# Decode attention and MLP on one core: K and V loaded four heads at a time, P turned among zeros, a shorter MLP chain

## The chip, the cores and the metric

The kernel runs on one core of a Trainium2 chip. The metric is the device time of one execution in microseconds; the median of three runs before the change is 203.85 us (202.43 to 204.0). All data starts and ends in HBM.

## The reference

One decode step for 8 sequences: a layer norm, attention over the last 2048 keys of a cache with 8 key heads (each shared by 4 query heads of 128), an output projection, and a two-part mixer and MLP. With sequence length 1, each of the four token shifts of the mixer moves its quarter of `h` out of range, so the term `hs` is zero, and `w1` and `w2` don't matter.

```python
W = min(4096, max(256, Sk // 4))           # 2048 of 8192 keys
q = (x @ wq) ...                            # 8 x 32 heads x 128
scores = einsum("bhqd,bhkd->bhqk", q, k) * Dh ** -0.5
o = einsum("bhqk,bhkd->bhqd", softmax(scores), v)
A = o.reshape(B, 1, 4096) @ wo

h  = x + A(layernorm(x))
u  = layernorm(h)                           # B's input
x1 = u                                      # the shifted term is zero
h2 = gelu(layernorm(x1) @ w3) @ w4          # 512 -> 1792 -> 512
out = h + x1 + h2
```

## The kernel before

**Items.** K and V are read once: 8 sequences x 8 key heads are 64 items, each with 512 KB of K and 512 KB of V. An item is loaded as 128 partitions of 4 KB (`load_k`, L362, `load_v`, L367): partition p holds the 16 consecutive keys 16p to 16p+15. There are `NK = 11` slots for K and `NV = 13` for V. All these loads go through SP's queue, and wait there for the turn (K) or the PV (V) that last used the slot.

**Turn and scores.** TensorE turns an item's K in 16 transposes of 128x128 (`pe_T`, L252) into one of two PSUM buffers; ACT copies the lower half to SBUF and VectorE the upper (`evict`, L260 and L262). `pe_QK` (L270) then runs four matmuls side by side on the four column groups, each with 32 stationary columns (`qblk`: four columns of this head's queries, the others zero) and 512 keys as moving columns. The 8 heads of a sequence accumulate into one PSUM tile `S_ps`: partitions are 4 quarters of keys times 32 query heads, columns 512 keys.

**Softmax.** After a sequence's eighth QK come the maximum over the columns (L279), a transpose of that to one row by a matmul (L283), the maximum over quarters and its negation (L285, L288), a matmul that turns it back into a column (L292), and Exp on ACT with the row sums beside it (L296, one instruction on 128 partitions x 512). Four transposes (L305) turn P, VectorE copies it (L309), and a matmul with ones adds up the row sums (L317), of which VectorE takes reciprocals (L319, L324).

**PV.** `pe_PV` (L331) runs 16 matmuls per item, V chunks as stationary operand and four columns of P as moving one. A sequence's heads 0 to 6 are scaled together into `oK` (L341), turned by four small matmuls against a selection matrix (L353) and copied to `o2` (L358); head 7 is scaled straight into `o2` (L345). The next sequence's PV waits for that copy, since it uses the same PSUM bank. In the last sequence each head has its own bank, its own turn, and its part of the output projection (`pe_wo`, L383, which starts with x as first summand).

**Order.** One loop over p (L391) writes the order out for every engine: turn p, then one of the softmax steps, then QK of item p-2, then PV of item p-13, with the loads of K p and V p-13 on SP. wo comes in five loads between items 15 and 39. After the loop SP has w3 and w4 (w4 in two parts, 1 KB runs).

**MLP (L459 to L522).** h lies transposed, 128 partitions of 4 x 8 columns. The mean comes from a fp32 matmul with ones and a reduction, h is centred, squared, and summed the same way. Two Sqrt on ACT and two reciprocals give both norms (the second norm of a norm is one factor: L470). u goes through w3 in two halves (L486), each followed by gelu written out in five DVE steps and a Tanh, then w4 (L508), the last sum, a transpose, a copy and the store.

Of the kernel before, what the change touches and what calls it, by code (L numbers as in the profile page):

```python
# [6 lines left out]
dt = mybir.dt  # L7
# [4 lines left out]
B = 8  # L12
D = 512
# [15 lines left out]
NK = 11  # L29
NV = 13  # L30
NKT = 4
LQK = 2
LV = 13
WO_AT = (15, 23, 31, 39)
# [32 lines left out]
def bass_sequential_preLN__sliding_block_cached__mixer_s_mlp__decode_kernel(  # L67
# [19 lines left out]
    NITEM = NB * G  # L87
# [3 lines left out]
    with es:  # L91
# [3 lines left out]


        iota_f = sb([128, 128], dt.float32, "iota_f")
# [3 lines left out]
        ones_f = sb([128, 128], dt.float32, "ones_f")  # L101
        scratch = sb([128, 2], dt.float32, "scratch")
        eps1 = sb([128, 1], dt.float32, "eps1")
        eps2 = sb([128, 1], dt.float32, "eps2")
# [8 lines left out]
        wbig = sb([128, KC * H * DH], dt.bfloat16, "wbig")  # L113
        wq_v = wbig[:, :].rearrange("p (k n) -> p k n", k=KC)

        wo_v = wbig[:, :].rearrange("p (g k n) -> p g k n", g=G, k=R)
        w3_sb = sb([128, KC, F], dt.bfloat16, "w3_sb")
        w4_sb = sb([128, FC, D], dt.bfloat16, "w4_sb")

        qblk = sb([128, B, G, H], dt.bfloat16, "qblk")  # L120
        knat = sb([128, NK, NC * DH], dt.bfloat16, "knat")
        vnat = sb([128, NV, NC * DH], dt.bfloat16, "vnat")
        kT_sb = sb([128, NKT, W], dt.bfloat16, "kT_sb")

        P_sb = sb([128, 2, 512], dt.bfloat16, "P_sb")
        pT_sb = sb([128, 2, NC, H], dt.bfloat16, "pT_sb")
# [7 lines left out]
        GL = G - 1  # L134
# [3 lines left out]
        oK = sb([128, G, R, R], dt.bfloat16, "oK")  # L138
# [3 lines left out]
        hs = sb([128, NH], dt.float32, "hs")  # L142
        hc = sb([128, NH], dt.float32, "hc")
        hsq = sb([128, NH], dt.float32, "hsq")
        msum = sb([128, B], dt.float32, "msum")
        vsum = sb([128, B], dt.float32, "vsum")
        s1 = sb([128, B], dt.float32, "s1")
        s2 = sb([128, B], dt.float32, "s2")
        r1 = sb([128, B], dt.float32, "r1")
        r2 = sb([128, B], dt.float32, "r2")  # L150
        xb = sb([128, NH], dt.float32, "xb")
        fin = sb([128, NH], dt.float32, "fin")
        uT = sb([128, NH], dt.bfloat16, "uT")
        g_x = sb([128, FC * B], dt.float32, "g_x")
        g_q = sb([128, FC * B], dt.float32, "g_q")
        g_t = sb([128, FC * B], dt.float32, "g_t")
        gT = sb([128, FC * B], dt.bfloat16, "gT")
        fT = sb([128, NH], dt.bfloat16, "fT")
# [3 lines left out]

# [3 lines left out]
        pT_ps = sm[:, 0:256].bitcast(dt.bfloat16)  # L166
# [6 lines left out]
        sem_v = [S(f"sem_v{i}") for i in range(NV)]  # L173
        sem_x, sem_wq, sem_wo, sem_w3, sem_w4a, sem_w4b, sem_out = (
# [8 lines left out]

# [3 lines left out]
        PO.op(lambda e: e.memset(eps1[:], EPS))  # L187
        e_eps = PO.op(lambda e: e.memset(eps2[:], EPS * EPS))
        e_iota = PO.op(lambda e: e.iota(iota_f[:], [[1, 128]], base=0, channel_multiplier=-1,
                                        allow_small_or_imprecise_dtypes=True))  # L190
        e_ones = PO.op(lambda e: e.memset(ones_f[:], 1.0))
        e_qz = PO.op(lambda e: e.memset(qblk[:], 0.0))
        e_warm = AC.op(lambda e: e.activation(scratch[:, 1:2], scratch[:, 0:1], ACT.Exp), e_scr)

        e_idb = DV.op(lambda e: e.tensor_single_scalar(ident_b[:], iota_f[:], 0.0, ALU.is_equal), e_iota)
        e_idf = DV.op(lambda e: e.tensor_single_scalar(ident_f[:], iota_f[:], 0.0, ALU.is_equal))
# [6 lines left out]
        e_sel = DV.op(lambda e: e.tensor_reduce(sel_f[:, :], ident_f[:, :].rearrange("p (q h) -> p h q", q=4),  # L203
# [6 lines left out]

        def pe_xT(e):
            for kc in range(KC):
                ins = e.matmul(pT_ps[:, kc * B:(kc + 1) * B],  # L213
                               xln_b[:, :].rearrange("b (p k) -> b k p", k=KC)[:, kc, :],
                               ident_b[0:B, 0:B], is_transpose=True)
            return ins
        e = PE.op(pe_xT, e_xln, e_idb)
        e_xT = DV.op(lambda e: e.tensor_copy(xlnT[:, :], pT_ps[:, 0:KC * B]), e)
# [11 lines left out]
        def dve_q(e):  # L230
            for g in range(G):
                ins = e.tensor_scalar(qblk[:, :, g, R * g:R * (g + 1)],  # L232
                                      S_ps[0][:, R * g * B:R * (g + 1) * B].rearrange("p (i b) -> p b i", b=B),
                                      inv_sqrt_dh, None, ALU.mult)
            return ins
        e_qblk = DV.op(dve_q, e_q, e_qz)


        e_Tlo, e_Thi, e_lo, e_hi, e_QK, e_PV = {}, {}, {}, {}, {}, {}
        e_max, e_mT, e_neg, e_negps, e_negc, e_exp, e_PT, e_pT, e_lsel, e_Lb, e_rL, e_scale, e_sc = ({} for _ in range(13))  # L240

        def K(i):
            return sem_k[i % NK], 16 * (i // NK + 1)

        def V(i):
            return sem_v[i % NV], 16 * (i // NV + 1)

        def pe_T(i):
            def half(lo):
                def f(e):  # L250
                    for c in range(lo, lo + NC // 2):
                        ins = e.matmul(kT_ps[i % 2][:, c * 128:(c + 1) * 128],  # L252
                                       knat[:, i % NK, c * DH:(c + 1) * DH], ident_b[:, :], is_transpose=True)
                    return ins
                return f
            e_Tlo[i] = PE.op(half(0), K(i), e_lo.get(i - 2), e_idb)
            e_Thi[i] = PE.op(half(NC // 2), e_hi.get(i - 2))

        def evict(i):
            e_lo[i] = AC.op(lambda e: e.activation(kT_sb[:, i % NKT, 0:W // 2], kT_ps[i % 2][:, 0:W // 2], ACT.Copy),  # L260
                            e_Tlo[i], e_QK.get(i - NKT))
            e_hi[i] = DV.op(lambda e: e.tensor_copy(kT_sb[:, i % NKT, W // 2:W], kT_ps[i % 2][:, W // 2:W]),  # L262
                            e_Thi[i], e_QK.get(i - NKT))

        def pe_QK(i):
            b, g = divmod(i, G)

            def f(e):
                for q in range(4):
                    ins = e.matmul(S_ps[b % 2][32 * q:32 * (q + 1), :], qblk[:, b, g, :],  # L270
                                   kT_sb[:, i % NKT, 512 * q:512 * (q + 1)],
                                   start=(g == 0), stop=(g == G - 1),
                                   tile_position=(0, 32 * q), skip_group_check=True)
                return ins
            e_QK[i] = PE.op(f, e_lo[i], e_hi[i], e_qblk, e_exp.get(b - 2))


        def softmax_1(b):
            e_max[b] = DV.op(lambda e: e.tensor_reduce(mcol[:, :], S_ps[b % 2][:, :], AX.X, ALU.max),  # L279
                             e_QK[G * b + G - 1], e_mT.get(b - 1))  # L280

        def softmax_2(b):
            e_mT[b] = PE.op(lambda e: e.matmul(sm[0:1, MROW], mcol[:, :], ident_f[:, :], start=True, stop=True),  # L283
                            e_max[b], e_rL.get(b - 1), e_idf)
            e = DV.op(lambda e: e.tensor_reduce(Mrow[:, :], sm[0:1, MROW].rearrange("o (q h) -> o h q", q=4),  # L285
                                                AX.X, ALU.max), e_mT[b])
            m_bc = bass.AP(tensor=Mrow[:, :].tensor, offset=0, ap=[[H, 1], [0, 4], [1, H]])
            e_neg[b] = DV.op(lambda e: e.tensor_scalar(negrow[:, :].rearrange("o (q h) -> o q h", q=4), m_bc,  # L288
                                                       -1.0, None, ALU.mult), e, e_negps.get(b - 1))

        def softmax_3(b):
            e_negps[b] = PE.op(lambda e: e.matmul(sm[:, NEG], negrow[0:1, :], ones_f[0:1, 0:1],  # L292
                                                  start=True, stop=True), e_neg[b], e_ones)
            j = b % 2
            e_negc[b] = DV.op(lambda e: e.tensor_copy(negcol[:, j:j + 1], sm[:, NEG]), e_negps[b], e_exp.get(b - 2))  # L295
            e_exp[b] = AC.op(lambda e: e.activation(P_sb[:, j, :], S_ps[j][:, :], ACT.Exp, bias=negcol[:, j:j + 1],  # L296
                                                    scale=1.0, accum_out=lcol[:, j:j + 1]),
                             e_negc[b], e_PT.get(b - 2), e_lsel.get(b - 2))

        def softmax_4(b):  # L300
            j = b % 2

            def f(e):
                for jt in range(4):
                    ins = e.matmul(pT_ps[:, jt * 128:(jt + 1) * 128], P_sb[:, j, 128 * jt:128 * (jt + 1)],  # L305
                                   ident_b[:, :], is_transpose=True)
                return ins
            e_PT[b] = PE.op(f, e_exp[b], e_negc[b])
            e_pT[b] = DV.op(lambda e: e.tensor_copy(  # L309
                pT_sb[:, j, :, :].rearrange("p (q jt) h -> p q jt h", jt=4),  # L310
                pT_ps[:, 0:NC * H].rearrange("p (jt q h) -> p q jt h", jt=4, q=4)),
                e_PT[b], e_PV.get(G * (b - 2) + G - 1))
            e_lsel[b] = DV.op(lambda e: e.tensor_scalar(lsel[:, :], sel_f[:, :], lcol[:, j:j + 1], None, ALU.mult),
                              e_Lb.get(b - 1), e_sel)

        def softmax_5(b):
            e_Lb[b] = PE.op(lambda e: e.matmul(sm[:, LB], ones_f[:, :], lsel[:, :], start=True, stop=True),  # L317
                            e_lsel[b], e_pT[b])
            e_r = DV.op(lambda e: e.reciprocal(rL[:, b % 2, :], sm[:, LB]), e_Lb[b],  # L319
                        e_scale.get(b - 2))  # L320
# [236 lines left out]
```

## Time and profile before

| | |
|---|---|
| median of three runs | 203.85 us |
| the profiled execution | 202.54 us |
| its span, first to last instruction | 201.1 us |
| mean granted TensorE clock | 0.829 |
| TensorE matmul busy | 156.3 us (78%) |
| VectorE, ACT busy | 76.5, 79.5 us |
| HBM read | 79.18 MB, 394 GB/s over the span |
| K transposes (L252), 1024 | 80.7 us busy |
| PV (L331), 1024 | 35.8 us busy |
| QK (L270), 256 | 30.2 us busy, four side by side |

A busy time of TensorE counts pipelined instructions whole, so it says when the engine is in use, not how close to its peak it is. The granted clock is the share of full speed that the clock throttle let through. A chain of waits is followed back from the last instruction, at each step to what released it; its lines are a start, a duration, an engine and a line.

### The profile page before, as it was taken

To read this page: it belongs to the slowest core of one execution; us is meant where nothing else is said; L and a number is where in the kernel's file an instruction comes from. 1 tells how busy PE (TensorE), PEld (TensorE's weight loads), DVE (VectorE), ACT (ScalarE), POOL (GpSimd) and SP (SyncE) were. 2 spreads that over 40 slices of the span, in tenths; PEclk is the share of its full clock that TensorE was granted. 3 is DMA by queue.
4 is the path that set the end of the run, shared out by engine and by line. 5 is a ranking of instruction groups with operands and counts; after the bars stand their busy time and mean duration, and the time that the engine had idled before them with its cause. 6 is when DMAs were issued, how large, how long until landed. Compare 5 with 4: busy or idle time off the path is not lost.

```text
span 201.1 us, 6188 instructions
## 1 busy us (share of the span) xinstructions
PE 156.3 (78%) x2821; PEld 126.0 (63%) x2821; DVE 76.5 (38%) x204; ACT 79.5 (40%) x91; POOL 2.5 (1%) x10
## 2 busy tenths in 40 slices
PE   0039999897876987678974898879798878979754
PEld 0039776676755765565863676657676666769753
DVE  6103556534441335213352246233524333234143
ACT  6003778744532444423432436444534523240030
POOL 4000000000000000000000000000000000000000
PEclk9999999999978797975799669996969975755555
DMA  6989999999999999999999999999999999999950
GB/s 223 476 364 418 420 416 421 415 415 418 416 420 416 421 415 415 421 416 420 418 409 413 420 417 419 417 416 418 417 420 416 415 420 421 415 418 416 393 179 2
DMA packets 22506, 79.59 MB, mean 396 GB/s; under 512 B 2248, under 2 KB 4560, under 8 KB 22352
## 3 DMA queue, kind: packets, MB, share of 16 engines
q1 hardware_dynamic: 22464, 79.18, 97.1%
q8 instruction: 22, 0.36, 0.6%
q10 hardware_dynamic: 16, 0.01, 0.0%
q14 instruction: 4, 0.03, 0.0%
HBM read 79.18 MB, written 0.01 MB: 394 GB/s over the span
## 4 chain that ended last, share of the span: by engine, by line
DMA 50%; PE 38%; DVE 6%; ACT 2%; issue 2%
DMA knat<-in_A_k_cache_dram 44%; PE kT_ps L252 19%; DMA wbig<-in_A_wq_dram 6%; PE S_ps L270 5%; PE oT_ps L331 4%; PE S_ps L383 2%; PE S_ps L225 2%; DVE kT_sb L262 1%; PE kT_ps L331 1%; PE sm L305 1%; PE sm L292 1%; ACT P_sb L296 1%; PE sm L283 1%; DVE mcol L279 1%; ACT L296 1%
## 5 line engine op out<-in xcount | busy, mean ns | idle before, releaser
L260 ACT ACTIVATE kT_sb<-kT_ps 128x1024 bf16<-128x1024 bf16 x64 | 65.5, 1023 | 95.1 <-PE kT_ps L252 95.0
L252 PE MATMUL kT_ps<-ident_b,knat 128*128 128x128 bf16 x1024 | 80.7, 243 | 12.0 <-DMA knat<-in_A_k_cache_dram 11.8
L252 PEld LDWEIGHTS kT_ps<-ident_b,knat 128*128 128x128 bf16 x1024 | 69.4, 110 | 16.7 <-DMA knat<-in_A_k_cache_dram 13.9
L262 DVE COPY kT_sb<-kT_ps 128x1024 bf16<-128x1024 bf16 x64 | 44.3, 692 | 92.7 <-PE kT_ps L252 92.6
L331 PEld LDWEIGHTS oT_ps<-pT_sb,vnat 128*128 128x128 bf16 x896 | 26.9, 98 | 27.4 <-issue 18.4
L331 PE MATMUL oT_ps<-pT_sb,vnat 128*128 128x4 bf16 x896 | 31.4, 165 | 11.2 <-DVE o L358 6.3
L270 PE MATMUL S_ps<-kT_sb,qblk 128*32 128x512 bf16 x256 | 30.2, 433 | 0.0
L270 PEld LDWEIGHTS S_ps<-kT_sb,qblk 128*32 128x32 bf16 x256 | 7.4, 95 | 5.6 <-issue 1.6
L225 PE MATMUL S_ps<-xlnT,wbig 128*128 128x8 bf16 x128 | 3.6, 168 | 7.7 <-DMA wbig<-in_A_wq_dram 7.7
L225 PEld LDWEIGHTS S_ps<-xlnT,wbig 128*128 128x128 bf16 x128 | 3.5, 104 | 7.8 <-issue 7.8
L296 ACT ACTIVATE P_sb<-S_ps,negcol 128x512 bf16<-128x512 f32 x8 | 5.5, 687 | 6.2 <-DVE negcol L295 6.2
L279 DVE TENSOR_REDUCE mcol<-S_ps 128x1 f32<-128x512 f32 x8 | 5.5, 682 | 1.4 <-PE S_ps L270 1.4
L470 ACT ACTIVATE s<-vsum,eps 128x8 f32<-128x8 f32 x1 | 0.3, 301 | 13.7 <-DVE vsum L467 13.7
L232 DVE TENSOR_SCALAR qblk<-S_ps 128x32 bf16<-128x32 f32 x8 | 0.9, 182 | 10.8 <-PE S_ps L225 10.8
L305 PE MATMUL sm<-ident_b,P_sb 128*128 128x128 bf16 x32 | 3.6, 242 | 1.7 <-ACT P_sb L296 1.7
L331 PE MATMUL kT_ps<-pT_sb,vnat 128*128 128x4 bf16 x128 | 4.4, 166 | 0.0
L383 PE MATMUL S_ps<-o,wbig 128*128 128x8 bf16 x128 | 4.4, 169 | 0.0
L213 PE MATMUL sm<-ident_b,xln_b 8*128 8x8 bf16 x4 | 0.3, 174 | 5.1 <-DVE xln_b L201 5.1
L309 DVE COPY pT_sb<-sm 128x512 bf16<-128x512 bf16 x8 | 3.3, 417 | 2.3 <-PE sm L305 2.3
L331 PEld LDWEIGHTS kT_ps<-pT_sb,vnat 128*128 128x128 bf16 x128 | 4.0, 104 | 0.1
L383 PEld LDWEIGHTS S_ps<-o,wbig 128*128 128x128 bf16 x128 | 3.9, 105 | 0.1
L283 PE MATMUL sm<-ident_f,mcol 128*1 128x128 f32 x16 | 3.7, 317 | 0.4 <-DVE mcol L279 0.3
(82 smaller groups left out, 72.5 us busy)
## 6 DMA issues: line engine op xcount, KB each, us to landing
knat<-in_A_k_cache_dram SPq DMA_DIRECT2D x64, 512.0 KB, 15.2
vnat<-in_A_v_cache_dram SPq DMA_DIRECT2D x64, 512.0 KB, 15.3
wbig<-in_A_wq_dram SPq DMA_DIRECT2D x1, 4096.0 KB, 12.3
wbig<-in_A_wo_dram SPq DMA_DIRECT2D x3, 1024.0 KB, 16.0
w_sb<-in_B_w_dram SPq DMA_DIRECT2D x1, 1792.0 KB, 16.8
w_sb<-in_B_w_dram SPq DMA_DIRECT2D x1, 1280.0 KB, 19.7
wbig<-in_A_wo_dram SPq DMA_DIRECT2D x2, 512.0 KB, 14.6
w_sb<-in_B_w_dram SPq DMA_DIRECT2D x1, 512.0 KB, 17.3
```

The costliest lines, as they stand in the source:

```text
L225: ins = e.matmul(S_ps[0][:, h * B:(h + 1) * B], wq_v[:, kc, h * DH:(h + 1) * DH], xlnT[:, kc * B:(kc + 1) * B], start=(kc == 0), stop=(kc ...
L252: ins = e.matmul(kT_ps[i % 2][:, c * 128:(c + 1) * 128], knat[:, i % NK, c * DH:(c + 1) * DH], ident_b[:, :], is_transpose=True)
L260: e_lo[i] = AC.op(lambda e: e.activation(kT_sb[:, i % NKT, 0:W // 2], kT_ps[i % 2][:, 0:W // 2], ACT.Copy), e_Tlo[i], e_QK.get(i - NKT))
L262: e_hi[i] = DV.op(lambda e: e.tensor_copy(kT_sb[:, i % NKT, W // 2:W], kT_ps[i % 2][:, W // 2:W]), e_Thi[i], e_QK.get(i - NKT))
L270: ins = e.matmul(S_ps[b % 2][32 * q:32 * (q + 1), :], qblk[:, b, g, :], kT_sb[:, i % NKT, 512 * q:512 * (q + 1)], start=(g == 0), stop=(g ...
L279: e_max[b] = DV.op(lambda e: e.tensor_reduce(mcol[:, :], S_ps[b % 2][:, :], AX.X, ALU.max), e_QK[G * b + G - 1], e_mT.get(b - 1))
L283: e_mT[b] = PE.op(lambda e: e.matmul(sm[0:1, MROW], mcol[:, :], ident_f[:, :], start=True, stop=True), e_max[b], e_rL.get(b - 1), e_idf)
L296: e_exp[b] = AC.op(lambda e: e.activation(P_sb[:, j, :], S_ps[j][:, :], ACT.Exp, bias=negcol[:, j:j + 1], scale=1.0, accum_out=lcol[:, j:j ...
L305: ins = e.matmul(pT_ps[:, jt * 128:(jt + 1) * 128], P_sb[:, j, 128 * jt:128 * (jt + 1)], ident_b[:, :], is_transpose=True)
L309: e_pT[b] = DV.op(lambda e: e.tensor_copy(pT_sb[:, j, :, :].rearrange("p (q jt) h -> p q jt h", jt=4), pT_ps[:, 0:NC * H].rearrange("p (jt ...
L331: ins = e.matmul(dst, vnat[:, i % NV, c * DH:(c + 1) * DH], pT_sb[:, b % 2, c, R * g:R * (g + 1)], start=(c == 0), stop=(c == NC - 1))
L383: ins = e.matmul(hT_ps[:, nb * B:(nb + 1) * B], wo_v[:, g, k, nb * 128:(nb + 1) * 128], o2[:, g, k, :], start=False, stop=(g == GL and k = ...
```

## The change

**Loads.** The unit is now four key heads of one sequence (`NU = 2` units per sequence, 16 in all, 2 MB of K and 2 MB of V each). Partition 4r+j of a slot holds 64 consecutive keys (16 KB) of head j of the unit. There are four slots for K and four for V; `load_v` of a unit is issued behind `load_k` of the unit three later. The last V unit comes in four quarters. wo comes in four loads of 1 MB. w3 and w4 no longer have tiles of their own: they go to K slots 0 and 1 once those are turned, w4 with 14 consecutive rows per partition. So that gelu's rows fit these, w3's stationary operands take every fourteenth column (`w3_c`).

**Scores.** A unit is worked in four blocks u of 16 chunks of 128 columns (64 blocks in all). A turned chunk now has four heads' keys side by side, every fourth column one head's, so each column group takes one head, and its moving operand steps by four columns. The stationary operand is a window of 32 columns cut from a tile `qz` with four query columns between two stretches of 28 zeros; where the window is cut puts the four rows where this block's scores belong.

**Softmax and PV.** Exp is four ACT instructions, one per head group of 32 partitions, that write every fourth column of a tile `Pz` that is zero elsewhere. `Pz` is turned by 16 transposes in the same two PSUM buffers as K, and ACT and VectorE copy it as they copy K. A PV matmul then takes 16 columns of that (four heads x four query heads) against a V chunk that holds four heads' keys. PV of block i is at loop step i+14. `oK` and `o2` are made per unit (`scale`, `turn_o`), wo in two calls.

**MLP.** The sum over the four column groups is now one reduction ahead of a single matmul with -1/D; w3 is applied to centred h straight away, and the norm's factor is multiplied in behind w3. The variance matmul runs between the halves of w3, and the two factors are made by a power of -0.5 on POOL. gelu is one ACT instruction per half; a dummy gelu ahead of the MLP loads its table.

```diff
-NK = 11
-NV = 13
+NU = 2
+J = G // NU
+U = 4
+RR = 32
...
+NK = 4
+NV = 4
 LQK = 2
-LV = 13
-WO_AT = (15, 23, 31, 39)
+LV = 14
+LVD = 3
+WO_AT = (5, 7, 9, 11)
+QW = 28 + R + 28
...
+        w3_sb = knat[:, 0, 0:KC * F].rearrange("p (k f) -> p k f", k=KC)
+        w4_sb = knat[:, 1, 0:FC * D].rearrange("p (c n) -> p c n", c=FC)
...
+        def turn16(src, dst, *waits, free=()):
+            k = len(e_Tlo)
+            prev = lambda l: l[k - 2] if k >= 2 else None
...
+            e_Tlo.append(PE.op(part(0), prev(e_lo), e_idb, *waits))
+            e_Thi.append(PE.op(part(8), prev(e_hi)))
+            e_lo.append(AC.op(lambda e: e.activation(dst[:, 0:1024], kT_ps[k % 2][:, 0:1024], ACT.Copy),
+                              e_Tlo[k], *free))
+            e_hi.append(DV.op(lambda e: e.tensor_copy(dst[:, 1024:2048], kT_ps[k % 2][:, 1024:2048]),
+                              e_Thi[k], *free))
...
+                for j in range(J):
+                    ins = e.matmul(S_ps[b % 2][32 * j:32 * (j + 1), :].rearrange("p (c r) -> p c r", c=16),
+                                   qz[:, b, J * t + j, lo:lo + 32],
+                                   kT_sb[:, i % NKT, :].rearrange("p (c r j) -> p j c r", c=16, j=J)[:, j],
...
+                for j in range(J):
+                    q = slice(32 * j, 32 * (j + 1))
+                    ins = e.activation(Pz[q, s, :].rearrange("p (c r j) -> p j c r", c=16, j=J)[:, j],
+                                       S_ps[s][q, :].rearrange("p (c r) -> p c r", c=16), ACT.Exp,
+                                       bias=negcol[q, s:s + 1], scale=1.0, accum_out=lcol[q, s:s + 1])
...
+            e_PT[b], e_pS[b] = turn16(Pz[:, s, :], pS[:, s, :], e_exp[b],
+                                      free=(e_PV.get(NU * U * (b - 1) - 1),))
+            e_lsel[b] = DV.op(lambda e: e.tensor_scalar(lsel[:, :], sel_f[:, :], lcol[:, s:s + 1], None, ALU.mult),
+                              e_exp[b], e_Lb.get(b - 1), e_sel)
...
+                for c in range(16):
+                    o = c * 128
+                    mvg = pS[:, b % 2, o:o + 128].rearrange("p (j x h) -> p x j h", j=J, h=R)[:, 2 * w + t]
+                    ins = e.matmul(dst, vnat[:, n % NV, (16 * w + c) * DH:(16 * w + c + 1) * DH], mvg,
+                                   start=(w == 0 and c == 0), stop=(w == U - 1 and c == 15),
+                                   skip_group_check=True)
...
+            e_PV[i] = PE.op(f, V(n, w), *e_pS[b], e_sc.get(n - 1))
...
+        def load_k(n):
+            b, t = divmod(n, NU)
+            dma(SP, knat[:, n % NK, :],
+                A_k_cache[b, J * t:J * (t + 1), W0:SK, :].rearrange("j (r c) d -> r j (c d)", r=RR), sem_k[n % NK],
+                e_T.get(U * (n - NK + 1) - 1))
...
+        e_gl = AC.op(lambda e: e.activation(scratch[:, 1:2], scratch[:, 0:1], ACT.Gelu_apprx_tanh), e_warm)
...
+        dma(SP, w3_sb, B_w3.rearrange("(k p) f -> p k f", p=128), sem_w3, e_T[U * (NUN - NK + 1) - 1])
+        w4_src = B_w4.rearrange("(p c) n -> p c n", c=FC)
...
+        e_hsum = DV.op(lambda e: e.tensor_reduce(hsum[:, :], vr(hT_ps[:, 0:NH]), AX.X, ALU.add), e_wo[-1])
+        e_hs = DV.op(lambda e: e.tensor_copy(hs[:, :], hT_ps[:, 0:NH]))
+        st1, st2 = sm[:, 0:B], oT_ps[:, 0:B]
+        e_mu = PE.op(lambda e: e.matmul(st1, ones_m[:, :], hsum[:, :], start=True, stop=True), e_hsum, e_ones, sm_read[0])
+        e_hb = DV.op(lambda e: e.tensor_tensor(v3(hb[:, :]), v3(hs[:, :]), bc(st1), ALU.add), e_mu, e_hs)
...
+        w3_c = w3_sb.rearrange("p k (m c) -> p k c m", c=FC)
...
+                        ins = e.matmul(y_ps[n][:, f * B:(f + 1) * B], w3_c[:, kc, n * FH + f, :],
...
+            if n == 0:
+                e = PE.op(lambda e: e.matmul(st2, ones_v[:, :], vsum[:, :], start=True, stop=True), e_vs, e_sc[NUN - 1])
+                DV.op(lambda e: e.tensor_scalar(vv[:, 0:B], st2, 1.0 + EPS, EPS * EPS, ALU.mult, ALU.add), e)
+                e_vv = DV.op(lambda e: e.tensor_scalar(vv[:, B:2 * B], st2, EPS, None, ALU.add))
+                e_rr = PO.op(lambda e: e.tensor_tensor(rr[:, :], vv[:, :], half[:, :], ALU.pow), e_vv)
...
+            e = DV.op(lambda e, n=n, cs=cs: e.tensor_tensor(v3(g_x[:, cs]), v3(y_ps[n][:, 0:FH * B]),
+                                                            bc(rr[:, 0:B], FH), ALU.mult), e_y[n], e_rr)
+            e_gT.append(AC.op(lambda e, cs=cs: e.activation(gT[:, cs], g_x[:, cs], ACT.Gelu_apprx_tanh), e))
```

## The prediction, made before the change was run

> **What bounds the kernel now.** I read the page's slices first: is any resource full all the time?
>
> ```profile
> PE   0039999897876987678974898879798878979754
> ...
> PEclk9999999999978797975799669996969975755555
> DMA  6989999999999999999999999999999999999950
> ```
>
> DMA is full from the second slice to the 38th; TensorE is nearly full, at a clock that falls to half in places. Next, the chain of waits from the landing that freed the third-last K chunk:
>
> ```profile
> 148.54 15.98 DMA knat<-in_A_k_cache_dram
> 164.56 1.90 PE kT_ps L252 x16
> ...
> 174.99 0.36 PE S_ps L270 x4
> 175.37 0.70 DVE mcol L279
> ...
> 177.93 0.79 ACT P_sb L296 x2
> ...
> 178.76 0.62 PE sm L305 x4
> 179.41 0.42 DVE pT_sb L309
> ...
> 189.74 1.39 PE S_ps L383 x48
> ```
>
> So the end is set in two steps: the stream of K until 164.5, then 36.6 us in which the last batch's scores (until 175.36), softmax, PV, wo and the MLP follow one another on TensorE, DVE and ACT. V and the weights, which land later, cost at most small waits. The windows of 3.41 us, cut where the granted clock changes (busy PE, PEld, DVE, ACT, POOL, then clock, DMA share, GB/s), show when TensorE slows:
>
> ```profile
> 40.38:43.79 3.41, 3.41 (x76) 2.75 (x74) 1.34 (x3) 2.05 (x2) 0.00 (x0) 1.00 1.04 422
> 54.03:57.45 3.41, 2.00 (x42) 1.69 (x43) 1.72 (x7) 1.02 (x1) 0.00 (x0) 1.00 1.03 421
> 57.45:60.86 3.41, 3.41 (x50) 2.78 (x47) 0.69 (x1) 1.02 (x1) 0.00 (x0) 0.50 1.03 421
> 173.50:176.91 3.41, 3.10 (x78) 2.15 (x74) 1.46 (x4) 0.00 (x0) 0.00 (x0) 1.00 1.03 420
> 176.91:180.32 3.41, 2.48 (x43) 2.23 (x40) 1.12 (x6) 2.06 (x3) 0.00 (x0) 0.50 1.02 416
> ```
>
> A thin window is followed by one at half clock; a window filled by transposes brings the clock back. From 176.9 to the end all is at half.
>
> **The stream.** The trace's packet records give 159 ns for a 4 KB packet and 1213 ns for wq's 32 KB ones; wq's start 1209.5 ns apart on each engine. The steady 418 GB/s make 156.8 ns per 4 KB. A line through 156.8 and 1209.5 gives about 608 ns for 16 KB, against 627 for four of 4 KB: 3.1% faster, and no row lies between, so the bounds are 0 and 3.6% (the 32 KB rate). Before, wq (4.19 MB) landed at 13.04, and the 164.52 landing needed 61.9 MB more (62 K and 48 V chunks of 0.524 MB, wo's 4.19): 408.5 GB/s, the slowest engine included. After, the last K unit needs 28 units of 2.10 MB and wo, 62.9 MB: 58.7 MB at 408.5 x 1.031 is 139.4, wo 10.3; it lands at 13.0 + 149.7 = 162.7. Slots hold 8 units, 39 us of stream, so SP's waits on turns and on PV don't starve it. w4's and w3's edits, and V's last unit in quarters, lie behind that landing; the weights would land near 188 and are first needed at 190.
>
> **But the last landing now brings four chunks.** TensorE then owes, at full clock: 64 K transposes 4.0 (1.00 per 16 from the chain), batch 6's P transposes 1.0 (16, not 4, at the same 62 ns), six QK at 0.33, five PV at 0.48, two small matmuls 0.35: 9.7 us. At half (1.80, 1.80, 0.55, 0.50, 0.85 in the same order) 15.6. In between units it has work of 8.0 to 8.7 us against 9.7 us of stream, so gaps, thin windows, and some half clock. I take one and a half half-clock windows plus a short wait for ACT's Exp, 12.3: the last scores end at 175.0, against 175.36. That eats the stream's gain.
>
> QK now reads kT_sb with a step of 8 bytes; no row shows such a read. Bounds: 0.33 us per chunk as now, or double. I take 0.33, nearest in shape. Double costs 2 us in the last unit and 2.6 per batch before.
>
> The Trainium skill, SBUF — State Buffer, section "Door 1: The DMA port swizzle", says that 16-byte lines hit twice or more are read at full rate, and that each access to a new line pays. By it the 0.33 stands (an 8-byte step hits a line twice), and w3's loads below, with a step of 28 bytes, pay; no run here shows either yet.
>
> **Softmax of the last batch.** Until the negated maximum is in place nothing changes: 2.57 us. Exp becomes four ACT instructions on 32 partitions, each with as many columns as the one before (687 ns, the next op 0.68 after it): 4 x 0.68 + 0.1 = 2.8, against 0.83. In mid-stream that adds about 2 us between exp and P's transposes; there TensorE waits behind it with QK, PV and the next turn, but a unit's spare 1.0 to 1.7 us and ACT's 60% idle time cover most. At the end nothing does. Then 16 P transposes at half clock 1.9, VectorE's half of the copy 0.69 (ACT's 1.02 starts sooner), lsel queued behind it 0.2, the sum matmul 0.65, and a PV of batch 6 queued behind that, 0.5: 4.0 with hand-overs, against 1.99 (178.76 to the first PV at 180.75).
>
> **PV and wo of the last batch.** Eight PV at 0.50, 132 wo matmuls 4.4, and the waits for oK and o2 twice, 1.6 (VectorE 0.2 to 0.27 each plus hand-over): 10.0, against 10.38, which held 1.30 of "issue". PV has 16 columns where it had 4; the nearest row, wo's 8 columns, is 0.52 against 0.42 to 0.49, so up to 1.2 more. What is saved mid-stream is the 6.3 us for which PV waited on VectorE's o (L358), but that was time before the landing.
>
> **The MLP.** wo's end to w3's start: hsum 0.2, one fp32 matmul 0.65, hb 0.2, hand-overs: 1.2 instead of 3.36 (six more DVE and ACT steps and a second fp32 matmul). Behind w3's first half (0.93) the variance matmul 0.65, two DVE steps 0.4, the power on POOL, then one multiply and gelu 0.55, w4 in two parts 1.9, the last sums, turn and copy 0.85 as now. POOL has no such op in the trace: its rows run from 0.10 (128x1) to 1.8 (2048 columns); for 16 columns I take 0.5, near the iota's 0.24 plus hand-overs. w3's weight loads now step by 28 bytes (every fourteenth column). No row shows it: at least the 33 ns per load and matmul of now, at most the load's own 104 ns unhidden, 2.0 us more per half. I take 1.0 in all, nearer the hidden end, as these loads have always run ahead of the matmuls. Sum 7.95, against 8.54: 0.6 gained. The gelu table load falls behind Exp, as 1.28 us of idle ACT. POOL's larger memsets are done before 16 us.
>
> **Sum.** 175.0 + 2.57 + 2.8 + 4.0 + 10.0 + 7.95 + 1.42 (store, as now) = 203.7, against 201.1: 2.6 us longer. The profiled run took 202.54, 1.44 over its span, so 205.1; it lies 1.3 below the median of the three runs, 203.85, on which this is 206.4. I forecast 206.
>
> **Rivals.**
> Faster: TensorE meets the last unit at full clock and the softmax's transposes too. For it: windows full of transposes always regain the clock. Against: the end of before was at half throughout. Scores at 162.7 + 9.7 + 0.3 = 172.7, softmax 1.1 less, POOL's power at 0.2, w3's loads hidden: 199.0, so about 201.8 on the median; with 32 KB's rate 201.
>
> Slower, TensorE's clock: two-megabyte units leave gaps of over 1 us, then the last burst runs wholly at half, 15.6 plus 1 of backlog. It decides if over two windows of the last unit are at half; before had three in a row from 163.26. Scores at 179.3, end 208.0, on the median 210.8.
> The Trainium skill, TensorE: Matmul & The Clock Gate, section "Part 4: PE-mode transpose", says transposes don't count as activity. By it this rival is the likely one. The trace disagrees: of two windows with one QK group each, that of 118.89 (32 K transposes) kept the clock and that of 54.03 (16) lost it.
>
> Slower, the change doesn't do what it says: 16 KB packets bring nothing, since every engine now steps through four heads 2 MB apart. wq's 32 KB runs, 256 KB apart, speak against it. The landing comes 4.3 later: 208, on the median 210.8.
> The Trainium skill, DMA: Bandwidth & Descriptors, section "Latency and other measured facts", reports rates falling by a quarter at row pitches of 2 MiB; here the engines walk one head side by side, so I give it little; no run here shows it.
>
> **How the numbers follow.** Likeliest, as above: 0.45, own range 203 to 209. Faster rival 0.25, clock 0.2, no DMA gain 0.1. Under 1% (2 us) a measurement of this kernel can't tell from no change: 201.8 to 205.9 is the middle. The likeliest gives it 0.18, slower 0.25, faster 0.02; the faster rival 0.18 faster and 0.07 same; the others are slower. Faster 0.2, same 0.25, slower 0.55. The range reaches to the faster rival at 32 KB's rate with the softmax's waits a microsecond shorter, and to the clock rival with QK doubled in the last unit (2 us): 200 to 213.
>
> **What would show it.** The last K landing near 162.7 and 431 GB/s in steady windows; Exp as four rows of 687 ns; the last QK near 175; PV of the last unit's first head some 9.4 after that; w3 1.2 after wo. It is wrong if the last K lands after 165, if a group of four QK takes over 0.45 at full clock, or if the last unit takes less than 10 us or more than 15 from its landing to its last QK.

## The result, and the profile after

The changed kernel takes 230.19 us (median of four runs, 229.88 to 230.82), beside 203.93 for the kernel before (202.43 to 204.14): a ratio of 1.131, with a 95% interval of 1.125 to 1.137. The forecast was 206, with a range of 200 to 213. The sign was right, the size wrong by 24 us. The profiled execution took 229.88, its span is 228.6.

The slices of the page, in the same three rows as before:

```profile
PE   0068997299929992999299929992999399547883
...
PEclk9999999769985998899679976998599959955555
DMA  7989999999999999999999999999886506991000
```

DMA is no longer full to the end: it thins out after seven tenths of the span, from about 160 us. TensorE now has a hole (a digit of 2 among nines) every fourth slice, and the clock falls beside most of these. The page says the same as shares of the chain of waits: TensorE 64%, ACT 20%, DMA 7%; before, DMA had 50% and TensorE 38%. The chain itself, in one sequence in mid-stream and at the end:

```profile
60.66 0.69 DVE kT_sb L263
61.45 1.39 ACT Pz L314 x2
62.85 1.39 ACT Pz L314 x2
64.25 1.39 ACT Pz L314 x2
65.66 1.40 ACT Pz L314 x2
67.10 1.89 PE kT_ps L255 x16
68.99 0.55 PE S_ps L279 x4
...
195.07 0.70 DVE mcol L290
197.43 1.38 ACT Pz L314 x2
...
203.08 1.90 PE kT_ps L255 x16
205.01 0.69 DVE pS L263
...
217.58 0.61 PE sm L472 x2
218.45 1.84 PE kT_ps L486 x28
221.09 2.92 POOL Pz L494
224.59 1.67 PE S_ps L511 x56
```

Exp stands four times in it with 1.39 us, where the forecast had 0.68. This happens in every sequence: the first Exp rows start at 61.45, 84.98, 107.57 and so on, about 23.3 us apart, while the four units of a sequence come in every 4 x 4.89 = 19.6 us (429 GB/s, worked out from the spacing of the landings; 431 was forecast). What TensorE does meanwhile is in the groups (line, engine, operation, tiles, shapes, count, then busy us and mean ns of one, then idle time in front and what ended it). First three of the kernel before: Exp, P's transposes and QK.

```profile
L296 ACT ACTIVATE P_sb<-S_ps,negcol 128x512 bf16<-128x512 f32 x8 | 5.5, 687 | 6.2 <-DVE negcol L295 6.2
L305 PE MATMUL sm<-ident_b,P_sb 128*128 128x128 bf16 x32 | 3.6, 242 | 1.7 <-ACT P_sb L296 1.7
L270 PE MATMUL S_ps<-kT_sb,qblk 128*32 128x512 bf16 x256 | 30.2, 433 | 0.0
```

The same of the changed kernel, and the power on POOL:

```profile
L314 ACT ACTIVATE Pz<-S_ps,negcol 32x512 bf16<-32x512 f32 x32 | 44.4, 1387 | 6.1 <-DVE negcol L308 5.7
L255 PE MATMUL kT_ps<-ident_b,Pz 128*128 128x128 bf16 x128 | 15.1, 311 | 35.0 <-ACT Pz L314 35.0
L279 PE MATMUL S_ps<-kT_sb,qz 128*32 128x512 bf16 x256 | 41.1, 611 | 0.0
L494 POOL TENSOR_TENSOR Pz<-Pz,half 128x16 f32<-128x16 f32 x1 | 2.9, 2910 | 212.6 <-DVE Pz L493 212.6
```

Row by row: an Exp takes 1387 ns instead of 687; TensorE stands idle 35.0 us, 4.4 per sequence, in front of P's transposes, where it was 1.7 in all; a QK matmul takes 611 ns on average, where it took 433 (30.2 us for 256 before); POOL's power takes 2.91 us. The two means of QK mix two clocks. In windows at half clock four QK matmuls keep TensorE busy for 0.62 us in both kernels (57.45:60.86 before, 66.38:69.80 after); in windows at full clock for 0.40 before (54.03:57.45), but still for 0.62 after (from 60.85 to 61.47). So the stepped read costs nothing extra at half clock, and half as much again at full clock. TensorE's wait for K's landings, 1.2 us in all, is gone as a bound. By the packet records the last K unit landed at about 163, as forecast (162.7), but its last QK ended 32 us later, at 195.07; the forecast had 12.3.

The windows of 3.41 us around the wait at 62 to 67 (start:end, length, then busy PE, PEld, DVE, ACT, POOL, granted clock, DMA share, GB/s):

```profile
62.97:66.38 3.41, 0.09 (x2) 0.00 (x0) 0.69 (x1) 3.38 (x5) 0.00 (x0) 1.00 1.03 437
66.38:69.80 3.42, 2.70 (x32) 2.06 (x33) 0.77 (x2) 2.71 (x4) 0.00 (x0) 0.50 0.98 414
69.80:73.21 3.41, 3.41 (x50) 2.90 (x48) 1.31 (x4) 1.02 (x1) 0.00 (x0) 0.50 1.00 428
73.21:76.62 3.41, 3.41 (x62) 2.32 (x58) 1.36 (x3) 1.92 (x2) 0.00 (x0) 1.00 1.05 442
```

The window in which TensorE does next to nothing is followed by two at half clock, in which P's 16 transposes take 1.89 us and the next turn 1.72, against 0.91 to 1.00. Of the seven such holes in mid-stream six are followed by two windows at half clock and one (86.86) by one. So a wait of 4.4 us costs about 6.1, as an estimate from these rows: the wait, and some 1.7 for the two slow turns.

### The profile page after: what moved, and what is told of

Same layout as the page of the kernel before. It is cut to its first block, busy times and chain, and to the rows that moved or that the text cites. A ratio compares the mean times of both kernels' runs of the same rounds, so it can differ in the third digit from the quotient of the medians.

```text
span 228.6 us, 6312 instructions
## 1 busy us (share of the span) xinstructions
PE 171.3 (75%) x2925; PEld 131.6 (58%) x2925; DVE 81.3 (36%) x192; ACT 124.4 (54%) x145; POOL 10.8 (5%) x14
## 4 chain that ended last, share of the span: by engine, by line
PE 64%; ACT 20%; DMA 7%; DVE 4%; issue 2%; POOL 1%; SPq 0%; DVEq 0%
PE kT_ps L255 33%; ACT Pz L314 19%; PE S_ps L279 14%; PE oT_ps L353 11%; DMA knat<-in_A_k_cache_dram 7%; DVE kT_sb L263 2%; PE S_ps L410 2%; POOL Pz L494 1%; PE sm L328 1%; PE kT_ps L486 1%; PE sm L294 1%; PE S_ps L511 1%; ACT L314 1%; DVE mcol L290 0%; DVE pS L263 0%
## 5 line engine op out<-in xcount | busy, mean ns | idle before, releaser
L255 PE MATMUL kT_ps<-ident_b,knat 128*128 128x128 bf16 x1024 | 74.1, 231 | 1.2 <-DMA knat<-in_A_k_cache_dram 1.2
L314 ACT ACTIVATE Pz<-S_ps,negcol 32x512 bf16<-32x512 f32 x32 | 44.4, 1387 | 6.1 <-DVE negcol L308 5.7
L353 PEld LDWEIGHTS oT_ps<-pS,vnat 128*128 128x128 bf16 x1024 | 30.5, 98 | 22.7 <-issue 22.6
L255 PE MATMUL kT_ps<-ident_b,Pz 128*128 128x128 bf16 x128 | 15.1, 311 | 35.0 <-ACT Pz L314 35.0
L279 PE MATMUL S_ps<-kT_sb,qz 128*32 128x512 bf16 x256 | 41.1, 611 | 0.0
L353 PE MATMUL oT_ps<-pS,vnat 128*128 128x16 bf16 x1024 | 35.7, 171 | 1.1 <-DVE oK L363 1.1
L255 PEld LDWEIGHTS kT_ps<-ident_b,Pz 128*128 128x128 bf16 x128 | 13.0, 145 | 36.3 <-ACT Pz L314 36.3
L279 PEld LDWEIGHTS S_ps<-kT_sb,qz 128*32 128x32 bf16 x256 | 7.3, 94 | 5.5 <-issue 1.4
L261 ACT ACTIVATE pS<-kT_ps 128x1024 bf16<-128x1024 bf16 x8 | 8.2, 1024 | 1.7 <-PE kT_ps L255 1.1
L314 ACT ACTIVATION_READ_ACCUMULATOR Pz<-S_ps,negcol 32x1 f32 x32 | 7.9, 248 | 0.0
## 6 DMA issues: line engine op xcount, KB each, us to landing
wbig<-in_A_wq_dram SPq DMA_DIRECT2D x1, 4096.0 KB, 12.3
```

What stands on the lines that cost most here:

```text
L255: ins = e.matmul(kT_ps[k % 2][:, c * 128:(c + 1) * 128], src[:, c * DH:(c + 1) * DH], ident_b[:, :], is_transpose=True)
L261: e_lo.append(AC.op(lambda e: e.activation(dst[:, 0:1024], kT_ps[k % 2][:, 0:1024], ACT.Copy), e_Tlo[k], *free))
L279: ins = e.matmul(S_ps[b % 2][32 * j:32 * (j + 1), :].rearrange("p (c r) -> p c r", c=16), qz[:, b, J * t + j, lo:lo + 32], kT_sb[:, i % NK ...
L314: ins = e.activation(Pz[q, s, :].rearrange("p (c r j) -> p j c r", c=16, j=J)[:, j], S_ps[s][q, :].rearrange("p (c r) -> p c r", c=16), AC ...
L353: ins = e.matmul(dst, vnat[:, n % NV, (16 * w + c) * DH:(16 * w + c + 1) * DH], mvg, start=(w == 0 and c == 0), stop=(w == U - 1 and c == 15),
```

## The experiments

Two things were open: why an Exp of the same 512 columns takes twice as long, and how much of the 26 us each of Exp, QK and the MLP brings. Each of the first four kernels ran once, on a chip where the kernel before took 203.49; what they gain is counted from the changed kernel's 230.19. Runs of one kernel lie up to 3 us apart here.

**Exp writes side by side.** Each head's Exp writes 512 elements in a row; everything else is as in the changed kernel. P's keys then stand in other places, so the product is not the reference's, but the instructions are as many and as large.

```diff
-ins = e.activation(Pz[q, s, :].rearrange("p (c r j) -> p j c r", c=16, j=J)[:, j],
-                   S_ps[s][q, :].rearrange("p (c r) -> p c r", c=16), ACT.Exp,
+ins = e.activation(Pz[q, s, 512 * j:512 * (j + 1)], S_ps[s][q, :], ACT.Exp,
```

> The four Exp instructions write their 512 columns side by side instead of every fourth column; P is then turned with its keys in other places (the product is not the reference's, the work the same). Theory A, the step of 8 bytes in Exp's output makes it 1387 ns: it falls to 687 ns each, a batch's four to 2.8 us, TensorE's 35.0 us of waiting for Exp falls to about 13, and the run takes 230 - 22 - 3 (the last batch's, with nothing beside it) = 205 to 210 us, the lower end set by the stream of K. Rival B, 32 partitions at a time or the accumulated sums make it slow: 1387 ns stays, and 230 us. Rival C, Exp's wait hides another one (QK or evictions): Exp falls, the time stays over 222 us.

Measured: 210.67 us, 19.5 less. The groups of that run:

```profile
L314 ACT ACTIVATE Pz<-S_ps,negcol 32x512 bf16<-32x512 f32 x32 | 21.7, 678 | 6.0 <-DVE negcol L308 5.7
L255 PE MATMUL kT_ps<-ident_b,Pz 128*128 128x128 bf16 x128 | 12.5, 274 | 13.1 <-ACT Pz L314 13.1
```

With 32 partitions and elements side by side Exp costs 678 ns, so the number of partitions doesn't matter; the step of the writes does. TensorE's wait falls from 35.0 to 13.1 us, and DMA stays full to the end of the stream again.

**K turned in another order.** The turn uses a permuted identity, so that a turned chunk has each head's 32 keys side by side and QK reads runs of 64 bytes instead of every fourth column. Exp stays as in the changed kernel.

```diff
+e_perm = DV.op(lambda e: e.tensor_copy(perm_b[:].rearrange("p (j r) -> p j r", j=J),
+                                       ident_b[:].rearrange("p (r j) -> p j r", j=J)), e_idb)
...
-kT_sb[:, i % NKT, :].rearrange("p (c r j) -> p j c r", c=16, j=J)[:, j],
+kT_sb[:, i % NKT, :].rearrange("p (c j r) -> p j c r", c=16, j=J)[:, j],
```

> K is turned against an identity with its columns reordered, so that each head's 32 columns of a chunk lie side by side and QK reads runs of 64 bytes instead of a step of 8. If the step is what makes a group of four QK take 0.55 instead of 0.33 us, it is 0.33 to 0.38 again and the 64 groups save 11 to 14 us: 216 to 219 us. If QK is slow for another reason (four zero-padded windows, the clock), 0.55 and 230 us stay. If Exp alone sets the pace, QK falls and the wait for Exp grows by as much: 227 us or more.

Measured: 219.91, 10.3 less. QK is at its old price and Exp's wait is untouched:

```profile
L283 PE MATMUL S_ps<-kT_sb,qz 128*32 128x512 bf16 x256 | 29.3, 427 | 0.0
L259 PE MATMUL kT_ps<-ident_b,Pz 128*128 128x128 bf16 x128 | 15.1, 312 | 35.2 <-ACT Pz L318 35.2
```

**Both.** The two edits together.

> Both edits (Exp writes side by side, so not the reference's product; QK in runs). If the two together are what makes TensorE slower than the stream, DMA is full until the last K unit again, that unit lands near 163, the last QK ends near 175 as in the forecast, and with the end of the kernel as measured (33.5 us after the last QK, less 2.8 of Exp) the run takes about 207 us. If another limit stands behind them (the P transposes, the order on TensorE), it stays above 213.

Measured: 208.2. The chain of waits of that run, at the end of the stream:

```profile
132.26 32.56 DMA knat<-in_A_k_cache_dram
...
175.49 0.36 PE S_ps L283 x4
175.87 0.70 DVE mcol L294
...
178.23 0.77 ACT Pz L318 x2
```

This is the kernel that the forecast priced: K lands at 164.82 (forecast 162.7), the last QK ends at 175.85 (175.0), Exp takes four times 0.77. Both edits together gain 22.0, not 19.5 + 10.3: TensorE again waits 15.1 us for K's landings, so the stream sets the pace once more.

**Exp spread out.** If the place of the Exp matters and not ACT's total, the slow Exp can stay: its four instructions are put between the copies of four turns, P's turn three steps later (not four, as the expectation has it), PV at i+17.

```diff
-LV = 14
+LV = 17
...
+if base + 2 <= p <= base + 5:
+    softmax_exp(b, p - base - 2)
```

> The four Exp instructions stay as they are, but one goes into each of four loop steps, between ACT's copies of K, and P is turned four steps later than now (PV three steps later). If it is the place of Exp in TensorE's order (a whole 5.6 us between two turns) that costs, the 35 us of waiting fall to about 6 (the last batch), and the run takes 203 to 212 us although Exp still takes 1387 ns. If ACT's total is the limit, the waits move to ACT's copies of K and the time stays over 222 us.

Measured: 211.88, 18.3 less, with Exp as slow as in the changed kernel and QK at 611:

```profile
L314 ACT ACTIVATE Pz<-S_ps,negcol 32x512 bf16<-32x512 f32 x32 | 44.8, 1399 | 6.8 <-DVE negcol L308 6.1
L255 PE MATMUL kT_ps<-ident_b,Pz 128*128 128x128 bf16 x128 | 10.2, 243 | 14.0 <-ACT Pz L314 14.0
```

TensorE's wait falls to 14.0 us and the granted clock rises from 0.839 to 0.903: between the first sequence's softmax and the last's only one window is at half. So ACT has the time; what costs is that four slow instructions in a row hold up P's turn, and with it all that TensorE's order puts behind it. The run moves two things, the Exp on ACT and P's turn on TensorE; what each brings by itself was not tried.

**The MLP's ends.** The changed kernel with w3 read side by side, w4 in 1 KB runs, and the power replaced by two Sqrt on ACT and a reciprocal on VectorE; gelu's table then loads behind the Sqrt.

```diff
-w3_c = w3_sb.rearrange("p k (m c) -> p k c m", c=FC)
+w3_c = w3_sb.rearrange("p k (c m) -> p k c m", c=FC)
...
-e_rr = PO.op(lambda e: e.tensor_tensor(rr[:, :], vv[:, :], half[:, :], ALU.pow), e_vv)
+AC.op(lambda e: e.activation(vv[:, 0:B], st2, ACT.Sqrt, bias=eps2[:, :], scale=1.0 + EPS), e)
+e_vv = AC.op(lambda e: e.activation(vv[:, B:2 * B], st2, ACT.Sqrt, bias=eps1[:, :], scale=1.0))
+e_rr = DV.op(lambda e: e.reciprocal(rr[:, :], vv[:, :]), e_vv)
```

> In the changed kernel, the norm's factors come from two Sqrt on ACT and a reciprocal on VectorE instead of a power on POOL, and w3's stationary operands are contiguous again (w4 back in 1 KB runs); its dummy activation loads the Sqrt table. By the trace after the change the power took 2.92 us and w3's first half 1.84 instead of 0.93; the Sqrt, the reciprocal and gelu's table load behind Sqrt (1.28) take about 1.9 in place of the power. If these two are what the MLP lost: 1.9 us less, 227.5 to 229. If gelu's table load doesn't overlap the reciprocal and the multiply: under 1 us less.

Measured: 227.53, one run, on a chip where the kernel before took 201.84, so the 2.7 to the changed kernel's median is loose. The traces are firmer: from w3's start to w4's it is 3.42 us (218.82 to 222.24) instead of 6.14 (218.45 to 224.59). w3's first half takes 0.91 instead of 1.84, and Sqrt (0.27 and 0.16) and a table load of 1.28 come in place of 2.92.

**One Exp, spread by VectorE.** With K's turn reordered and the MLP of the last run, one Exp over 128 partitions writes side by side, and two VectorE multiplies by a mask of four columns write it among zeros.

```diff
-for j in range(J): ...
+e.activation(P_sb[:, s, :], S_ps[s][:, :], ACT.Exp, bias=negcol[:, s:s + 1], ...)
+e.tensor_tensor(Pz[:, 0, 1024 * h:1024 * (h + 1)].rearrange("p (x j) -> p x j", j=J), s_bc, m_bc, ALU.mult)
```

> Everything of the change kept but its three slow forms: K turned in reordered columns (QK in runs), one Exp on 128 partitions written contiguously and spread among zeros by two VectorE multiplies of 128x1024 with a 0/1 mask, and the MLP of e5. Exp 0.69 us once per sequence, the multiplies about 1.1 us each. From e3's 206.9 us span: Exp 2.3 less, the multiplies 1.2 more on the path (the second half runs beside the first transposes), the MLP 2 less: span 203 to 204, time 204 to 206, even with before. If VectorE, which also copies half of K, gets late by the multiplies, K's copies wait and it stays at 207 or more.

Measured: 205.3, beside 201.84 for the kernel before on that chip, ratio 1.015 (1.008 to 1.022). The last QK ends at 175.46; the multiplies take 1.22 us each, 2.37 together on the path.

**Only the MLP.** The kernel before, its loads, turns, softmax and PV untouched, with the shorter MLP chain (Sqrt and reciprocal, w3 and w4 laid out as before, gelu in one instruction).

> The kernel before with the MLP of the change alone (w3 on centred h beside the variance, gelu in one op), w3 and w4 laid out as before, factors by Sqrt and reciprocal. Before, wo's end to the last transpose's end took 8.3 us. The new chain: reduction 0.2, mean matmul 0.65, hb 0.2, w3 0.93, variance 0.65, two Sqrt 0.5, gelu's table load 1.28 (reciprocal and multiply beside it), gelu 0.25, w4 1.9, end 0.85: 7.6. If that holds, 0.7 to 1.2 us faster than before: 0.4 to 0.6%. If the table load behind Sqrt costs all that was won: no change.

Measured: 200.67 (ten runs), ratio 0.993 (0.989 to 0.997): faster than both kernels, though than the one before by under 1%. In its trace the end of the last wo matmul to the end of the output's copy takes 7.6 us, as expected, against 8.5 before. Its chain shows what took over: not the MLP, but w3's landing.

```profile
172.87 18.92 DMA w_sb<-in_B_w_dram
191.92 0.89 PE kT_ps L477 x28
```

**The last K unit in quarters.** The kernel with one Exp, with that unit's load split in four and the small step for the row sums put ahead of P's copy.

```diff
+for w in range(U):
+    cs = slice(w * UL // U, (w + 1) * UL // U)
+    dma(SP, knat[:, n % NK, cs], src[:, :, cs], sem_kl[w], e_T.get(U * (n - NK + 1) - 1))
```

> e6 with two more edits: the last K unit comes in four quarters with a semaphore each, as V's last does, and the sums' lsel stands ahead of P's copy on VectorE. The first quarter lands 3.7 us before the unit, so TensorE starts its last four blocks that much earlier if it was waiting there (e3 waited for that landing); lsel first frees the sum matmul 0.9 us earlier. If so 3 to 4.5 us less than e6: 200 to 202.5 us, faster than before. If the backlog on TensorE, not the landing, sets the start of the last unit: under 1.5 us less.

Measured: 203.17 (ten runs), ratio 1.005 (1.002 to 1.008), 2.1 less than without, between the two expectations. What came instead is a wait for V, ahead of a softmax matmul in TensorE's order:

```profile
150.08 24.76 DMA vnat<-in_A_v_cache_dram
174.84 0.04 issue
174.89 0.56 PE oT_ps L366 x16
175.45 0.32 PE sm L314 x2
```

**Which step costs.** Each head's Exp has a step of its own, and QK reads every second column of the turned chunk (the kernel before took 201.36 on this chip). P and K's parts no longer belong together, so the product is not the reference's.

```diff
+e.activation(Pr[q[0], :, 0], S_[q[0], :]..., ACT.Exp, **kw[0])      # runs of 64 bytes, 256 apart
+e.activation(P2[q[1], :, 0], S_[q[1], :], ACT.Exp, **kw[1])         # every 2nd element
+e.activation(P3[q[2], :, 0], S_[q[2], :], ACT.Exp, **kw[2])         # every 3rd element
+e.activation(Pz[q[3], s, 0:512], S_[q[3], :], ACT.Exp, **kw[3])     # side by side
```

> The changed kernel with each head's Exp on a source line of its own and with another step of its writes: head 0 writes runs of 32 elements side by side (64 bytes, every fourth run), head 1 every second element (4 bytes), head 2 every third (6 bytes), head 3 side by side throughout; QK reads every second column of the turned chunk (4 bytes) instead of every fourth. P and K's parts no longer belong together, so the product is not the reference's; the count and size of all instructions are the same. Theory A (ACT pays for every write that does not lie right behind the one before, whatever the distance): heads 0 and 3 about 680 to 690 ns, heads 1 and 2 about 1390. Theory B (ACT writes a fixed number of bytes of a row at a time, and a step of 8 bytes spreads one such piece over two): the time grows with the step, head 1 at 690 to 1000, head 2 between it and 1390. Rival (each of the four slots of a batch has its price by its order or its partitions, not its step): all four equal, or the same as in the changed kernel's run, 1387. For QK: if the read costs by bytes spanned, a group of four at full clock falls from 0.55 to about 0.40 to 0.45; if any step costs alike it stays at 0.55; if a step of 4 bytes is free, 0.33. The whole: between 208 and 225.

```profile
L320 ACT ACTIVATE Pz<-S_ps,negcol 32x512 bf16<-32x512 f32 x8 | 8.8, 1102 | 0.1
L319 ACT ACTIVATE Pz<-S_ps,negcol 32x512 bf16<-32x512 f32 x8 | 6.6, 823 | 0.1
L321 ACT ACTIVATE Pz<-S_ps,negcol 32x512 bf16<-32x512 f32 x8 | 5.4, 679 | 0.1
L318 ACT ACTIVATE Pz<-S_ps,negcol 32x512 bf16<-32x512 f32 x8 | 5.4, 677 | 5.1 <-DVE negcol L308 5.1
...
L279 PE MATMUL S_ps<-kT_sb,qz 128*32 128x512 bf16 x256 | 29.4, 429 | 0.0
```

The run took 208.41 us. L318 to L321 are heads 0 to 3. Theory A falls: 4 bytes cost 823 and not 1390. Theory B holds in its numbers: 679 side by side, 823 at 4 bytes, 1102 at 6, 1387 at 8 (the last in the changed kernel), some 280 ns for each 2 bytes from 4 on. It isn't the space covered that costs: head 0's runs spread over as many bytes as the changed kernel's writes, and cost nothing extra. That a piece of a row is written at a time, as B says, is the explanation that fits; the runs show only the price by step. QK's read costs nothing extra at a step of 4 bytes (429 ns) and much at 8 (611), with nothing between tried.

**The variance ahead of w3.** The kernel before with the new MLP once more; the variance matmul, the two Sqrt and the reciprocal stand ahead of w3, where TensorE waits anyway.

> The kernel before with the MLP of the earlier run e7_before_mlp, and the variance's matmul, the two Sqrt and the reciprocal put ahead of w3 on TensorE, ACT and VectorE instead of behind w3's first half. There TensorE waits for w3's landing anyway (0.76 us in e7). Theory: the matmul (0.65) moves into that wait, so the end comes 0.3 to 0.65 us sooner than e7's 200.67: 200.0 to 200.4. Rival: the matmul needs the squares from ACT and VectorE, which are not there when TensorE begins to wait; then w3 stands behind that, and the time is 200.7 to 201.3.

Measured: 200.55 (twelve runs), ratio 0.994 (0.991 to 0.998), no different from the run without that (0.993). The timeline (start, duration, engine, line, operation, tiles, and in brackets the idle time and its releaser) shows why the time lies between the two expectations:

```profile
193.91 0.39 ACT L490 ACTIVATE gT<-g_x 128x56 bf16<-128x56 f32 x2
...
195.30 1.78 PEld L501 LDWEIGHTS S_ps<-gT,w_sb 128*128 128x128 bf16 x56 [1.68 <-ACT gT L490]
195.33 1.83 PE L501 MATMUL S_ps<-gT,w_sb 128*128 128x8 bf16 x56 [1.62 <-DMA w_sb<-in_B_w_dram]
```

gelu is done at 194.3, a microsecond sooner than without the edit (195.4), but w4's first part only lands at 195.2. The second lands at 196.5, and the last 16 matmuls of w4 start then (196.58). The stream is now the bound up to its last byte.

**PV later.** The kernel with the quartered K unit, PV at i+16 instead of i+14, and the variance first.

> e8_best with PV two steps later in TensorE's order (16 steps behind instead of 14), and the variance ahead of w3 as in e10. Theory: in e8 the sum and P's turn of the last batches stood behind PV that waited 1.2 us for V's landing; two steps later these wait behind nothing, so 1.0 to 1.3 us go, and up to 0.6 by the variance: 201.2 to 202.2, within 1% of the kernel before. Rival: the V landings are only met later, because the same PV must then be worked off after the softmax; the time stays at 203 or rises by up to 1 us, with the PV now on the chain after the last P turn.

Measured: 205.18, ratio 1.017 (1.012 to 1.023), where it was 1.005 with PV at i+14. The rival's course held, and by more than the 1 us that it allowed: the negated maximum came 0.34 us sooner (175.45 against 175.79), but more PV of the last sequence was left behind its softmax, and the last wo matmuls started 1.2 later (191.23 against 190.03). The two parts of the edit were not tried apart.

## Why the prediction was wrong

**The failed step** is the price of Exp: "each with as many columns as the one before (687 ns, the next op 0.68 after it): 4 x 0.68 + 0.1 = 2.8". The row was of an instruction that wrote side by side; the new one writes every fourth element. The same text gave QK's read with a step of 8 bytes a bound of double, and gave Exp's write with the same step none. It took 1387, and 678 when only the step was taken away.

The second half of that step failed with it. Four Exp were to add 2 us in mid-stream, which "a unit's spare 1.0 to 1.7 us and ACT's 60% idle time cover most". They cost four times 0.7 more than that, TensorE then stood 4.4 us per sequence, and half clock followed. ACT's idle time was there (the run with Exp spread out), but not at that place.

**QK** was taken at 0.33 for a group of four and cost 0.55, inside its stated bounds of 0.33 to 0.66. The Trainium skill, SBUF — State Buffer, section "Door 1: The DMA port swizzle", by which a step of 8 bytes reads at full rate, doesn't hold here, as the moving operand of four matmuls side by side: 611 ns against 427. For w3's step of 28 bytes it agrees: a weight load took 161 ns instead of 104.

Both together are TensorE's backlog (worth 19.5 us for Exp alone, 10.3 for QK alone, 22.0 for both): the last QK at 195.07 instead of 175.0, 20.1 of the 24.9 us by which the sum was short (a span of 228.6 against 203.7). The other terms: to the negated maximum 2.4 (2.57 forecast); Exp at the end 5.65 (2.8); from there to the first PV 4.5 (4.0); PV and wo 9.8 (10.0); the MLP 9.85 (7.95). Two of the signs of being wrong that the prediction named came up: a group of QK over 0.45 at full clock, and more than 15 us from the last unit's landing to its last QK (31.7).

**The MLP's term** was mis-sized at POOL's power: 2.91, outside its bounds of 0.10 to 1.8, for which 0.5 was taken. w3's steps cost 0.9 on the path, close to the 1.0 taken: the first half took 1.84 against 0.91 side by side, and the second, 1.80, ran beside the power.

**What held.** The stream (429 GB/s against 431) and the last unit's burst, once Exp and QK cost what was assumed: K's landing to last QK 11.0 us in the run with both edits, 12.3 forecast. That kernel took 208.2, within the likeliest case's own range of 203 to 209. The sign, slower, was thus right for more than the failed step: with Exp and QK at the prices assumed the kernel is still 4.7 us behind the one before on that chip, of which POOL's power, 2.4 over its term, is half. The faster rival never came: even with one Exp, QK at its old price and a better MLP the kernel stays level with or behind the one before, and by the traces the burst and the softmax behind it give back what the stream gains. The rival of TensorE's clock is not the cause: half clock is there, but behind the wait for Exp, and in mid-stream nearly goes when the Exp are spread. Two of the prediction's readings of the clock are weaker than they were put. The windows at 54.03 and 118.89 differ not in transposes alone: they hold 16 and 32 PV matmuls too (0.39 and 1.02 us), so they don't tell what counts for the clock. And from 13 us on in the profile before, the windows at full clock with TensorE busy for up to 2.18 of 3.41 us are all followed by half clock, but of the five with 2.25 to 2.30 only one is. The rival without DMA gain, whose landing would have come 4.3 us later, near 167, is out: K's last unit landed at about 163, and at 164.82 in the run with both edits.

## What to carry to other kernels

A duration belongs to an instruction with its access pattern: when an edit keeps the count of elements and changes their step, on either side, the old row is only a lower bound, and the same bound belongs on every engine that takes that step. A busy share says nothing about cover; ask what stands behind the slow instruction in each engine's written order. Of a change with many parts, try each alone: here the one part tried alone on the kernel before, the MLP, was the only one seen to help, by 0.7%.

## What the runs showed of the hardware

- ACT writing bf16 with a step: 679 ns for 512 columns side by side, 823 at 4 bytes, 1102 at 6, 1387 at 8; runs of 64 bytes are free (677).
- The moving operand of four side-by-side matmuls: 427 to 429 ns on average in runs of 64 bytes or at 4 bytes, 611 at 8. The difference is one of full clock alone: at half clock four of them keep TensorE busy for 0.62 us either way.
- A weight load of 128 columns with a step of 28 bytes: 161 ns against 104.
- A power of 128x16 fp32 on POOL: 2.91 us; two Sqrt (0.43 together) and a table load of 1.28, which hides the reciprocal, took its place in 1.7.
- In the run with the quartered K unit TensorE stops for 1.63 us of "issue" between two wo matmuls (190.64 to 192.27), and for 1.93 with PV later; in both a 16 KB packet of the instruction queue is under way as it begins (189.76 to 190.86, and 191.21 to 192.29). In the kernel before and in the run with one Exp, stops of 1.30 and 0.77 begin 0.2 and 0.5 after such a packet has ended, so the two need not belong together; what causes the stop stays open.
